# RetNet attention and a gated FFN on one core: the first batch's state is moved between partitions by two matrix products instead of two DMA copies

## The chip, the cores and the metric

The kernel runs on one core of a Trainium2 chip. A core has five instruction streams that run side by side and wait for each other through semaphores: TensorE (PE in the profile), VectorE (DVE), ScalarE (ACT), GpSimd (POOL) and SyncE (SP, which here only issues DMAs). Sixteen DMA engines move data between the chip's memory (HBM) and SBUF, the on-chip memory of 128 partitions. Matrix products are written to PSUM, which has eight banks.

The metric is device time in microseconds (us), as the median of several executions. Less is better.

## The reference

The reference computes a parallel RetNet attention for 8 batches of 8 heads (576 positions, 64 values per head), lays the result out as 4608 tokens of 512 values, and sends these through a gated feed-forward layer:

```python
def _attn_ref(q, k, v) -> np.ndarray:
    B, H, S, D_ = q.shape
    scale = 1.0 / np.sqrt(D_)
    scores = scale * np.matmul(q, k.transpose(0, 1, 3, 2))
    gamma = 1.0 - 2.0 ** (-5.0 - np.arange(H, dtype=np.float32))
    ...
    Dmat = np.where(rel >= 0, gamma[:, None, None] ** rel[None, :, :], 0.0)
    ret = scores * Dmat[None, :, :, :]
    return np.matmul(ret, v).astype(np.float32)
    ...
def _moe_ref(x, w_gate, w_val, w_out) -> np.ndarray:
    gate = 1.0 / (1.0 + np.exp(-(x @ w_gate)))
    val = x @ w_val
    return (gate * val @ w_out).astype(np.float32)
```

The feed-forward layer is 512 to 1536 to 512. The decay `gamma ** (i - j)` splits into a factor of the query's position and one of the key's, so attention can be done in chunks: inside a chunk by masked scores, and across chunks by a running state per head, the sum of k times v so far (64 x 64 values).

## The kernel before

**Attention.** The first chunks of batches 0 and 1 are done as "pairs" of 256 positions (`PAIRS`); everything after that as "steps" of 128 positions (`STEPS`), each of which loads `k`, `q` and `v` (256 KB each, lines 170 and 173), scales and casts them to bf16 (`cast_qk`, `cast_v`), turns q and k with a transposing DMA (`cross`, line 420), and makes scores (`scores`, L640), new shares of the state (`products`, L648), and values (`intra`, L666, and `inter`, L681, which multiplies by the state). A batch's last 64 positions are joined with those of the next batch in one step, in which `inter` reads the state of both batches after four chunks.

Batch 0's state is kept differently from the others'. The pairs keep it as a block matrix `sbd`: head 2m stands in partitions 0 to 63 and columns 0 to 63 of block m, head 2m+1 in partitions 64 to 127 and columns 64 to 127, with zeros elsewhere. The steps want head y*4+m in partitions half(y) and block m. `first_batch_state` makes the second form from the first, in a tile named `sf` in the profile: two quarters stay in their partitions and are copied by ACT, and two quarters change partitions and are copied by a DMA each, one issued on SP and one on ACT. It is called in `next_slot` for step 1. The step that reads the result is the last of batches 0 and 1, several steps later.

**Feed-forward.** The first 512 tokens are done while the weights still land (`h_both`, L1315, then `op_first`, L1465), the next 512 in two blocks of 256 (`h_units`, L884, `op_units`, L1225), and the other 3584 in blocks of 512 with a seven-product scheme (L1008 and L1123). The work of attention is put between the feed-forward products in an order that the kernel writes out by hand; each engine runs its list in order.

**Loads.** All loads go through a ring of landing tiles of 2 KB per partition (`landing`), and nearly all are issued on SP. The loads of pairs are in pieces of 512 bytes in SBUF, those of steps in pieces of 256 bytes (one head of one position), those of weights in pieces of 512 bytes for the first four, 1024 for the next four, and 2048 for the other sixteen and for `wo`. The order of issue in the first stage is: pairs 0 and 1, the gate and value weights, two loads of `wo`, `k` and `q` of pair 2, six of `wo`, `v` of pair 2 (`v32p`), four of `wo`. POOL casts that `v` into `vp` (L395), and TensorE's `pair_st` (L478) reads it.

**Places in SBUF.** Pools are laid out in the order in which they are opened. `lead` is the first and holds `blank`, `sbd[0]`, `trip` and `tri`, 1920 bytes per partition, from byte 16512 on; the landing tiles follow from byte 18432, and then all other pools; `consts` is the last.

Of the kernel before, what the change touches and what calls it, by code (L numbers as in the profile page):

```python
# [9 lines left out]
FP32 = mybir.dt.float32  # L10
BF16 = mybir.dt.bfloat16
# [5 lines left out]
def kernel(  # L17
# [19 lines left out]
    nc = tc.nc  # L37

    B, H, S, D = q.shape
    NT, DM = out.shape  # L40
    DFF = moe_w_gate.shape[1]
    P = 128
    M = H // 2
# [4 lines left out]
    lead = ctx.enter_context(tc.tile_pool(name="lead", bufs=1))  # L48
# [13 lines left out]
    st_psum = ctx.enter_context(tc.tile_pool(name="st_psum", bufs=1, space=PS))  # L62
# [44 lines left out]
    LAST = NC - 1  # L107
# [8 lines left out]
    NJ = P // 64  # L116
# [29 lines left out]
    def half(x):  # L146
        return slice(x * 64, x * 64 + 64)
# [16 lines left out]
    def load_part(s, i):  # L164

        b, c = STEPS[s]
        nm, src = (("k", k), ("q", q), ("v", v))[i]
        t = landing([P, H, D], f"{nm}32_{s}", s >= 8)
        if c < LAST:
            nc.sync.dma_start(out=t, in_=src[b, :, c * P:(c + 1) * P, :].rearrange("h p d -> p h d"))  # L170
        else:
            for j, (bj, tj) in enumerate(pieces_of(s)):
                nc.sync.dma_start(out=t[half(j)], in_=src[bj, :, tj:tj + 64, :].rearrange("h p d -> p h d"))
        loaded.setdefault(s, []).append(t)
# [93 lines left out]
    ident = consts.tile([P, P], BF16)  # L268
# [13 lines left out]
    sbd = [lead.tile([P, M, P], BF16, name="sbd0")]  # L282
# [6 lines left out]
    for p0 in (0, 64):  # L289
        nc.gpsimd.affine_select(out=trip[p0:p0 + 64], in_=trip[p0:p0 + 64], compare_op=ALU.is_ge, fill=0.0,  # L290
                                base=0, pattern=[[-1, 2], [1, P]], channel_multiplier=-2)
    tri = lead.tile([P, 64], BF16)

    def later_constants():

        nc.gpsimd.memset(tri, 1.0)
        for p0 in (0, 64):
            nc.gpsimd.affine_select(out=tri[p0:p0 + 64], in_=tri[p0:p0 + 64], compare_op=ALU.is_ge, fill=0.0,
                                    base=0, pattern=[[1, 64]], channel_multiplier=-1)
# [11 lines left out]
    on_pool, on_act, on_dve = nc.gpsimd.tensor_copy, nc.scalar.copy, nc.vector.tensor_copy  # L311
# [18 lines left out]
    def value_sums_begin():  # L330

        wt3_sb["w"] = []
        last = [sum_tile([P, 2, 2, 2 * P], BF16, f"wvt_{3 + i}", SUMS - 1 - i) for i in range(2)]
        for i in range(3):
            two = osb.tile([P, 2, 2, 2 * P], BF16, tag="osb", name=f"wvt_{i}")
            osb.held.append(osb.last)
            wt3_sb["w"].append([two[:, 0], two[:, 1], last[i // 2][:, i % 2]])
# [47 lines left out]
    def cast_pair(nm, A, g, eng):  # L385

        if (nm, A) not in natural:
            natural[nm, A] = osb.tile([P, 2, H, D], BF16, tag="osb", name=f"{nm}p_{A}")
        if nm != "v" and A == 2:
            o = natural[nm, A].rearrange("p r (m y) d -> p y m r d", y=2)[:, g]  # L390
        else:
            o = natural[nm, A][:, :, g * M:(g + 1) * M, :].rearrange("p r h d -> p h r d")
        i = parts.pop((nm, "pair", A, g))
        if nm == "v":
            eng(out=o, in_=i)  # L395
        else:
            tab = (ktab2 if nm == "k" else qtab2)[:, PAIRS[A][1], g * M:(g + 1) * M, :].unsqueeze(3).to_broadcast([P, M, 2, D])
            eng.tensor_tensor(out=o, in0=i, in1=tab, op=ALU.mult)
# [29 lines left out]
    state = {}  # L428
# [167 lines left out]
    def turn_step(s):  # L596

        t = att_pool.tile([P, 2, M, P], BF16, tag="T", name=f"T_{s}", bufs=6)
        for i, ((pool, tag), eng) in enumerate(zip(VALS, (on_act, on_dve))):
            ps = pool.tile([P, M, P], BF16, tag=tag, name=f"turn_{s}_{i}")  # L600
            for m in range(M):
                nc.tensor.matmul(ps[:, m, :], lhsT=natural_qk[s][:, i, m, :], rhs=ident, is_transpose=True,
                                 start=(m == 0), stop=(m == M - 1))
            eng(out=t[:, i], in_=ps)
        turned[s] = t
# [4 lines left out]
    def new_state(key, dt=BF16):  # L610
        final = dt == BF16 and key[1] == LAST - 1 and key[2] == NJ - 1
        tag = "s32" if dt == FP32 else "sf" if final else "sb"
        return nat_pool.tile([P, M, D], dt, tag=tag, name=f"{tag}_{key[0]}_{key[1]}_{key[2]}", bufs=8 if tag == "sb" else 5)

    def keep_state(key, src, eng):
        state[key] = new_state(key)
        eng(out=state[key], in_=src)  # L617
# [73 lines left out]
    def slot(s):  # L691

        if s > 0:
            val_ps[s - 1] = values(M, s - 1)
            intra(s - 1)
            inter(s - 1, [(0,), (1,)])
            mark(st_psum, "st")
        scores(s)
        if STEPS[s][1] < LAST:
            products(s)  # L700
        if s > 0:
            mark(st_psum, "st")
            inter(s - 1, [(1,), (0,)])
        mask(s)
# [74 lines left out]
    def after(s, i):  # L779

        makes = STEPS[s][1] < LAST
        to_bf16 = on_act if s < 6 else on_pool
        if i == 0:
            if makes:
                add_state(s, 0)
        else:
            if s > 0:
                leave_x(s - 1, i - 1)
                if i == 2 and dealt(cols_of(s - 1, 0)):
                    x_sums(at_col[s - 1], False)  # L790
            if i == 1 and makes:
                add_state(s, 1)
            if makes and (s, i - 1) in totals:
                b, c = STEPS[s]
                keep_state((b, c, i - 1), totals.pop((s, i - 1)), to_bf16)


    def first_batch_state():

        whole = new_state((0, LAST - 1, NJ - 1))  # L800
        for hh in range(2):
            for y in range(2):
                ((nc.sync, nc.scalar)[y].dma_start if hh != y else nc.scalar.copy)(
                    out=whole[half(y), hh::2, :], in_=sbd[3][half(hh), 2 * y:2 * y + 2, half(hh)])
        state[0, LAST - 1, NJ - 1] = whole

    pending = []

# [3 lines left out]
    def loads_to(n):  # L812
        while done["ld"] < min(3 * NS, n):
            load_part(*divmod(done["ld"], 3))
            done["ld"] += 1

    def casts_to(s):
        while done["cast"] <= min(NS - 1, s):
            x = done["cast"]
            loads_to(3 * (x + 1 + (AHEAD[x] if x < len(AHEAD) else 2)))  # L820
            cast_qk(x, 1, nc.gpsimd)
            cast_qk(x, 0, nc.vector if x < 2 else nc.gpsimd)
            if x not in TURNED:
                cross(x)
            cast_v(x, on_dve if x == 0 else on_pool)
            done["cast"] += 1
# [23 lines left out]

    def next_slot(s):
        slot(s)
        if s == 1:
            first_batch_state()
        casts_to(s + LEAD_CAST)
        for i in range(3):
            pending.append(lambda i=i: after(s, i))
        if s + 1 == 1:
            pending.insert(2, lambda: turn_step(s + 1))
# [463 lines left out]
    def step(units, n):  # L1323
        for _ in range(n):
            next(units)
# [88 lines left out]
    for i in range(2):  # L1414
        cast_w("g", 2, 2, i, on_pool)
    later_constants()
    cast_w("v", 2, 2, 0, on_pool)
    for i in range(4):
# [34 lines left out]
    step(units, 2)  # L1453
    cast_pair("q", 2, 1, nc.vector)
    step(units, 2)
    loads_to(6)
    value_sums_begin()
    for u in range(2):
# [65 lines left out]
    for w, (t0, n) in enumerate(BLOCKS):  # L1524
# [18 lines left out]
        for i, cols in enumerate(ffn_units(t0, n, nxt)):  # L1543
            if i in SUMS_AT.get(w, ()) and weight_sums:
                weight_sums.pop(0)()
            if w == 1 and i == n_h + TURN_AT:
                turn_step(7)
            for x in SPARE.get((w, i - n_h if w == 1 else i), ()):
                x()
            gone += cols  # L1550
            pieces += 1
            if stores and (nxt is None or w + 2 == len(BLOCKS) and pieces % 4 == 0):
                leave()
            if n > 256 and i % 2 and i < n_h:
                continue
            if pending:
                pending.pop(0)()
            elif slots < end and gone * (end - begin) >= (slots - begin) * (total - 5 * 2048):
                next_slot(slots)
                valued = slots - 1  # L1560
                slots += 1
            elif twos and (cue if n == 512 else i - n_h >= 1):
                cue.clear()
                next_two(*twos[0], n == 512)
                valued = twos[0][0][-1]
                slots = max([slots] + [s + 1 for s in twos.pop(0)[1]])
# [34 lines left out]
```

## Time and profile before

| | |
|---|---|
| median of 3 runs | 307.34 us (306.61 to 311.28) |
| the profiled execution | 309.1 us, of which the span of the instructions is 307.4 us |
| busy: PE, DVE, ACT, POOL | 298.5, 245.7, 196.9, 207.7 us |
| bytes moved by DMA | 55.01 MB, 179 GB/s over the span |
| granted clock of TensorE | 1.0 |

A row of a timeline gives the start and the duration in us, the engine, the line, the operation, the tiles written and read, and in square brackets the idle time of the engine before it and what ended it. "SPq" and "ACTq" are the engines' DMA issues. A row of the windows gives the stretch, its length, the busy time of PE, PEld, DVE, ACT and POOL with the number of instructions, the granted clock, the DMA share, and GB/s.

### The profile page before, as it was taken

The numbers are of one execution on the slowest core, as the hardware profiler recorded it, in microseconds if no ns is written. First come the engines' busy times: TensorE is split into PE (matmuls) and PEld (weight loads), VectorE is DVE, ScalarE is ACT, GpSimd is POOL, SyncE is SP. The second block draws the span as 40 slices with busy tenths as digits, with TensorE's granted clock in tenths as the row PEclk, the third lists the DMA queues.
The fourth block names the chain that finished last, engine by engine and source line by source line (L and its number), as shares of the span: only waits on it lengthen the run. The fifth ranks groups of instructions, "written<-read, shape, count | busy, mean of one in ns | idle before, by whom it ended". The sixth has DMA issues, their size and how long they took to land.

```text
span 307.4 us, 10860 instructions
## 1 busy us (share of the span) xinstructions
PE 298.5 (97%) x4442; PEld 244.2 (79%) x4442; DVE 245.7 (80%) x476; ACT 196.9 (64%) x422; POOL 207.7 (68%) x255
## 2 busy tenths in 40 slices
PE   8899999999999999999999999999999999999994
PEld 7774455876858788888888888888888888888883
DVE  5857695766889899789978997898789968945893
ACT  6765354454547746974797479757965796658640
POOL 5676463745476699769976997699669916751490
PEclk9999999999999999999999999999999999999999
DMA  7999999999999971999599919992880282013004
GB/s 211 315 295 393 341 322 229 216 200 180 228 202 263 227 167 38 233 231 231 133 226 254 177 38 214 228 211 41 211 200 2 61 282 75 2 52 90 0 3 137
DMA packets 144994, 55.01 MB, mean 179 GB/s; under 512 B 124336, under 2 KB 136880, under 8 KB 144944
## 3 DMA queue, kind: packets, MB, share of 16 engines
q1 hardware_dynamic: 144000, 53.64, 73.1%
q8 instruction: 35, 0.57, 0.8%
q10 hardware_dynamic: 944, 0.67, 0.8%
q14 instruction: 15, 0.12, 0.1%
HBM read 37.75 MB, written 9.44 MB: 154 GB/s over the span
## 4 chain that ended last, share of the span: by engine, by line
PE 68%; DMA 14%; DVE 8%; SPq 5%; issue 2%; POOL 1%; ACT 1%; ACTq 0%; DVEq 0%; POOLq 0%
PE gatea L1008 11%; PE wa L1008 10%; PE qa L1123 10%; PE qe L1123 7%; PE we L1008 5%; PE gatee L1008 5%; PE op L1225 3%; DMA wg<-in_moe_w_gate_dram 3%; SPq L184 3%; PE gateg L1008 3%; DMA q<-in_q_dram 3%; PE wg L1008 3%; DMA q32p<-in_q_dram 2%; PE h_v L884 2%; PE h_g L884 2%; DMA v32p<-in_v_dram 2%
## 5 line engine op out<-in xcount | busy, mean ns | idle before, releaser
L411 POOL TENSOR_TENSOR qk<-k,ktab 128x512 bf16<-128x512 f32 x30 | 32.2, 1073 | 16.0 <-DMA k<-in_k_dram 13.1
L1008 PEld LDWEIGHTS <-wg_sb 128*128 128x128 bf16 x336 | 32.8, 98 | 4.3
L1008 PEld LDWEIGHTS <-wv_sb 128*128 128x128 bf16 x336 | 32.9, 98 | 4.1 <-issue 0.3
L1123 PEld LDWEIGHTS <-gsum 128*128 128x128 bf16 x336 | 32.0, 98 | 4.9 <-DVE gsum L945 0.6
L945 POOL TENSOR_TENSOR gsum<-gv 128x256 bf16<-128x256 bf16 (+1 forms) x34 | 25.9, 769 | 12.4 <-DVE gv L1033 11.3
L411 POOL TENSOR_TENSOR qk<-q,qtab 128x512 bf16<-128x512 f32 x28 | 31.4, 1121 | 1.3 <-DMA q<-in_q_dram 1.3
L1008 PEld LDWEIGHTS <-wvt 128*128 128x128 bf16 x252 | 24.6, 98 | 3.9 <-issue 0.9
L1008 PEld LDWEIGHTS <-wgt_sb 128*128 128x128 bf16 x252 | 24.6, 98 | 3.7 <-issue 0.8
L1033 POOL TENSOR_TENSOR gv<-gv,wu 128x512 bf16<-128x512 bf16 x7 | 8.1, 1164 | 27.9 <-DVE wu L1059 27.9
L945 POOL TENSOR_TENSOR gsum<-gv,gsum 128x256 bf16<-128x256 bf16 x39 | 26.9, 720 | 0.0
L655 DVE TENSOR_TENSOR pt<-row,tri 128x256 bf16<-128x256 f32 x60 | 21.4, 412 | 6.6 <-PE val L681 3.1
L1123 PEld LDWEIGHTS <-gv 128*128 128x128 bf16 x240 | 23.0, 98 | 3.4 <-issue 0.4
L1008 PE MATMUL wa<-xsum,wv_sb 128*128 128x256 bf16 x168 | 25.2, 273 | 0.1
L1008 PE MATMUL gatea<-xsum,wg_sb 128*128 128x256 bf16 x168 | 24.1, 273 | 0.0
L617 ACT CAST sb<-s 128x256 bf16<-128x256 f32 x46 | 18.3, 413 | 6.3 <-DVE s L774 4.8
L742 ACT CAST xT<-val 128x256 bf16<-128x256 f32 x50 | 15.8, 388 | 6.6 <-PE val L681 6.6
L939 POOL TENSOR_TENSOR gsum<-gv 128x256 bf16<-128x256 bf16 (+1 forms) x16 | 14.5, 909 | 7.8 <-DVE gv L1033 7.8
L1054 DVE TENSOR_TENSOR gatee<-gatea,gs 128x512 f32<-128x512 f32 x14 | 9.8, 698 | 10.7 <-PE gatea L1008 7.4
L1033 POOL TENSOR_TENSOR gv<-gv,ws 128x512 bf16<-128x512 bf16 x14 | 16.3, 1164 | 2.6 <-DVE ws L1062 2.6
L1031 ACT ACTIVATE gv<-gs 128x512 bf16<-128x512 f32 x21 | 13.0, 630 | 7.8 <-DVE gs L1062 7.8
L1062 DVE TENSOR_TENSOR gs<-gatea,gs 128x512 f32<-128x512 f32 x21 | 13.8, 686 | 4.4 <-PE gatea L1008 3.6
L1062 DVE TENSOR_TENSOR ws<-wa,ws 128x512 f32<-128x512 f32 x21 | 14.4, 684 | 3.7 <-PE wa L1008 3.7
(181 smaller groups left out, 853.5 us busy)
## 6 DMA issues: line engine op xcount, KB each, us to landing
k<-in_k_dram SPq DMA_DIRECT2D x26, 256.0 KB, 4.2
q<-in_q_dram SPq DMA_DIRECT2D x26, 256.0 KB, 4.1
v<-in_v_dram SPq DMA_DIRECT2D x26, 256.0 KB, 4.3
out_dram<-ob SPq DMA_DIRECT2D x25, 256.0 KB, 3.1
wg<-in_moe_w_gate_dram SPq DMA_DIRECT2D x12, 256.0 KB, 5.1
wv<-in_moe_w_val_dram SPq DMA_DIRECT2D x12, 256.0 KB, 5.2
wo<-in_moe_w_out_dram SPq DMA_DIRECT2D x12, 256.0 KB, 5.1
v32p<-in_v_dram SPq DMA_DIRECT2D x6, 256.0 KB, 5.4
```

Of the source, the lines that this page charges most:

```text
L411: eng.tensor_tensor(out=natural_qk[s][:, i].rearrange("p m (y d) -> p y m d", y=2), in0=by_halves(loaded[s][1 - i]), in1=tab, op=ALU.mult)
L617: eng(out=state[key], in_=src)
L655: nc.vector.tensor_tensor(out=probs[s][:, y], in0=row_ps[s][y][:, 0], in1=tri.unsqueeze(1).to_broadcast([P, M, 64]), op=ALU.mult)
L742: nc.scalar.copy(out=x_out(ALL, cols_of(s, i)), in_=x_in(val_ps[s][i], cols_of(s, i)))
L884: nc.tensor.matmul(ps[:, i], lhsT=w_sb[:, kc, (fc + i) * P:(fc + i + 1) * P], rhs=xT(kc, slice(t0, t0 + n)), start=(kc == 0), stop=(kc == ...
L939: eng.tensor_tensor(out=s3, in0=a11, in1=a21, op=ALU.subtract)
L945: eng.tensor_tensor(out=to, in0=a, in1=b, op=op)
L1008: nc.tensor.matmul(ps[:, f], lhsT=w[:, kc, f * P:(f + 1) * P], rhs=x[:, kc], start=(first and f == 0 and kc == 0), stop=(f == 1 and kc == ...
L1031: nc.scalar.activation(out=to, in_=src, func=AF.Sigmoid)
L1033: eng.tensor_tensor(out=to, in0=to, in1=src, op=ALU.mult)
L1062: nc.vector.tensor_tensor(out=me["s5"], in0=a, in1=me["s5"], op=ALU.add)
L1123: nc.tensor.matmul(ps[:, b], lhsT=left(fp)[:, b * P:(b + 1) * P], rhs=right(fp), start=(first and fp == 0 and b == 0), stop=(fp == NFC // ...
```

## The change

A constant `stacked` of 128 x 192 is made on POOL in `later_constants`: zeros, with a 64 x 64 unit matrix in columns 64 to 127 of both halves of the partitions. Its columns 64 to 191 hold the unit matrices on the left (they add both halves of the input's partitions into the upper half of the output's), its columns 0 to 127 on the right (into the lower half). Two products with these, which add up in one PSUM tile `whole`, move the four quarters of `sbd[3]` to their places; the zeros of the block matrix add nothing. One ACT cast makes the bf16 tile `sf` of it. The function is called earlier: in the first 512 tokens, behind the last `h_both`, instead of in step 1.

```diff
     tri = lead.tile([P, 64], BF16)
+    stacked = lead.tile([P, 192], BF16)
 
     def later_constants():
 
+        nc.gpsimd.memset(stacked, 0.0)
+        for hh in range(2):
+            nc.gpsimd.tensor_copy(out=stacked[half(hh), 64:128], in_=ident[half(hh), half(hh)])
         nc.gpsimd.memset(tri, 1.0)
...
     def first_batch_state():
 
-        whole = new_state((0, LAST - 1, NJ - 1))
-        for hh in range(2):
-            for y in range(2):
-                ((nc.sync, nc.scalar)[y].dma_start if hh != y else nc.scalar.copy)(
-                    out=whole[half(y), hh::2, :], in_=sbd[3][half(hh), 2 * y:2 * y + 2, half(hh)])
-        state[0, LAST - 1, NJ - 1] = whole
+        ps = st_psum.tile([P, M, D], FP32, tag="st", name="whole")
+        for y in range(2):
+            nc.tensor.matmul(ps, lhsT=stacked[:, P - 64 * (y + 1):2 * P - 64 * (y + 1)], rhs=sbd[3][:, 2 * y:2 * y + 2, :],
+                             start=(y == 0), stop=(y == 1))
+        keep_state((0, LAST - 1, NJ - 1), ps, on_act)
...
         slot(s)
-        if s == 1:
-            first_batch_state()
         casts_to(s + LEAD_CAST)
...
     cast_pair("q", 2, 1, nc.vector)
     step(units, 2)
+    first_batch_state()
     loads_to(6)
     value_sums_begin()
```

With `stacked`, `lead` holds 2304 bytes, and the landing tiles begin at byte 18816 of each partition; all other tiles of the later pools move up by the same 384 bytes.

On ACT in step 1 before the change: the two copies of quarters, with the DMA issue between them, stand between the casts of the states `sb` and the sigmoid `gv`.

```order
L617 COPY sb_2_1_1263<-s_1_2_1_1224 128x256
L803 COPY sf_3_1_1353<-sbd_293 64x2x64
L803 DMA sf_3_1_1353<-sbd_293 64x2x64
L803 COPY sf_3_1_1353<-sbd_293 64x2x64
L887 ACTIVATE gv_1_1252<-h_g_6_1371 128x2x256
L762 COPY xT_1393<-val_0_1276 128x4x64
```

After the change the three are gone from there, and one cast stands much earlier on ACT, in the first 512 tokens, between the cast of a `wo` weight and the copies of pair 2's turned `k` and `q`:

```order
L318 COPY wo_sb<-wo_3_187 128x512
L621 COPY sf_3_1_856<-whole 128x256
L452 COPY kT_890<-kTp_0_885 128x512
L452 COPY qT_898<-qTp_0_893 128x2x2x128
L452 COPY kT_890<-kTp_1_902 128x512
L452 COPY qT_898<-qTp_1_910 128x2x2x128
```

So ACT loses two copies and a DMA issue in step 1 and has one cast more ahead of the four `kT` and `qT` copies. On SP in step 1 before the change, the other DMA copy stands between the transpose and the loads of step 5:

```order
L420 DMA_TRANSPOSE T_1197<-qk_1194 128x8x128
L803 DMA sf_3_1_1353<-sbd_293 64x2x64
L170 DMA k_5_1358<-in_k_dram 128x8x64
L170 DMA q_5_1360<-in_q_dram 128x8x64
L170 DMA v_5_1362<-in_v_dram 128x8x64
```

After the change the loads follow the transpose at once; nothing is put in the place of the DMA. On TensorE after the change, the two products stand behind the last product of `h_both` (`hv_11`) and ahead of the first of `op_first`:

```order
L1316 MATMUL hv_11_847<-xT_536,wv_sb 128x512
L806 LDWEIGHTS stacked
L806 MATMUL whole<-sbd_293,stacked 128x256
L806 LDWEIGHTS stacked
L806 MATMUL whole<-sbd_293,stacked 128x256
L1467 LDWEIGHTS gv_0_623
L1467 MATMUL op_0_881<-wo_sb,gv_0_623 128x512
```

Nothing else moves on TensorE. The line numbers after the change are up to 4 higher than before.

## The prediction

> **What bounds the kernel now.** I read the page's first two parts, then the windows by stage, the chain of waits, and the timelines around the two places that the change touches.
>
> ```profile
> PE 298.5 (97%) x4442; PEld 244.2 (79%) x4442; DVE 245.7 (80%) x476; ACT 196.9 (64%) x422; POOL 207.7 (68%) x255
> DMA  7999999999999971999599919992880282013004
> ```
>
> TensorE is busy for 97% of the span, so removing waits can win little. In the left third of the DMA row, up to about slice 14 of 40 (110 us), the DMA engines are as full as TensorE. The windows say this with numbers; the last two columns are the DMA share (mean busy share of 16 engines; overlapping packets can push it above 1) and GB/s.
>
> ```profile
> 1.00:19.00 18.00, 16.63 (x298) 14.04 (x299) 13.96 (x39) 12.36 (x24) 10.96 (x20) 1.00 0.96 282
> 19.00:45.00 26.00, 25.14 (x180) 12.84 (x179) 19.02 (x36) 13.66 (x26) 15.83 (x26) 1.00 1.02 347
> 60.00:88.00 28.00, 27.73 (x547) 20.92 (x537) 21.10 (x47) 12.74 (x31) 15.17 (x18) 1.00 1.10 205
> 5.00:10.00 5.00, 4.37 (x86) 3.66 (x86) 3.10 (x6) 3.05 (x6) 2.35 (x3) 1.00 1.10 321
> 25.00:30.00 5.00, 5.00 (x25) 2.25 (x23) 3.40 (x8) 3.51 (x6) 2.30 (x4) 1.00 1.06 404
> 80.00:85.00 5.00, 5.00 (x93) 4.51 (x79) 3.88 (x9) 2.47 (x6) 2.79 (x4) 1.00 1.09 246
> ```
>
> From 1 to 45 us the share is 0.96 and 1.02: no free DMA time. Where TensorE needs something that lands last in this stage, it waits, and the row shows it:
>
> ```profile
> 42.73 1.37 POOL L395 CAST vp<-v32p 128x512 bf16<-128x512 f32 x2 [0.58 <-DMA v32p<-in_v_dram]
> 43.40 0.19 PE L478 MATMUL st<-vp,kp 64*64 64x64 bf16 x1
> 44.15 0.31 PE L478 MATMUL st<-vp,kp 64*64 64x64 bf16 x9 [0.56 <-POOL vp L395]
> ```
>
> So until 44 us the end is set by how fast bytes land, after that by TensorE with the DMA close behind. The granted clock is 1.00 in every window.
>
> **The change, the small terms.** *TensorE.* Two products of 256 columns are added behind the last `hv`. From the chain of waits, and the timelines of TensorE and ACT:
>
> ```profile
> 81.41 0.87 PE h_g L884 x8
> 42.69 0.64 PE L457 MATMUL qkp<-qT,kT 64*64 64x128 bf16 x32
> 38.80 0.62 ACT L314 CAST wo_sb<-wo 128x512 bf16<-128x512 f32 x1 [3.42 <-DMA wo<-in_moe_w_out_dram]
> 40.86 0.76 ACT L448 COPY qT<-qTp 128x512 bf16<-128x512 bf16 x1
> ```
>
> Eight such products take 0.87 us, so two take 0.22. They stand ahead of the wait of 0.56 us for `vp` at 43.40, which covers them: 0. Without that cover they cost 0.22. *ACT there.* The new cast of `whole` is queued behind the `wo` cast that ends at 39.42 and ahead of four copies of `kT` and `qT`. From the page's groups, POOL's groups and POOL's timeline:
>
> ```profile
> L617 ACT CAST sb<-s 128x256 bf16<-128x256 f32 x46 | 18.3, 413 | 6.3 <-DVE s L774 4.8
> 20.30 0.52 POOL L298 TENSOR_SCALAR_AFFINE_SELECT tri<-tri 64x64 bf16<-64x64 bf16 x2
> L288 POOL MEMSET trip<- 128x256 bf16 x1 | 0.3, 337 | 0.0
> 22.89 1.23 POOL L309 CAST wg_sb<-wg 128x512 bf16<-128x512 f32 x2 [0.76 <-DMA wg<-in_moe_w_gate_dram]
> ```
>
> A cast of this shape takes 0.41, so the last copy ends at 42.03 instead of 41.62, still before the products at 42.69 that read it: 0. *POOL.* A memset of 192 columns (the 256-column one took 0.34) and two copies of 64x64 (the row of two 64x64 selects took 0.52): at most 0.9 us at 20.07. POOL then waits 0.76 us for a weight at 22.13, so at most 0.14 us is handed on, and the casts behind it wait for DMA again; should the cover fail, 0.9 us less the 0.56 at `vp` is 0.3. *The old place.* Here the change takes something away; timelines of ACT, TensorE and SP:
>
> ```profile
> 59.40 0.30 ACT L803 COPY sf<-sbd 64x128 bf16<-64x128 bf16 x1
> 61.04 0.71 ACTq L803 DMA_DIRECT2D sf<-sbd  x1
> 61.79 0.29 ACT L803 COPY sf<-sbd 64x128 bf16<-64x128 bf16 x1 [2.10 <-DMA T<-qk]
> 63.31 0.59 ACT L887 ACTIVATE gv<-h_g 128x512 bf16<-128x512 f32 x1
> 63.80 0.36 ACT L762 CAST xT<-val 128x256 bf16<-128x256 f32 x1
> 61.84 1.04 PE L884 MATMUL h_g<-xT,wg_sb 128*128 128x256 bf16 x8
> 63.72 0.22 PE L666 MATMUL val<-pt,v 64*64 64x64 bf16 x2
> 64.21 0.31 PE L666 MATMUL val<-pt,v 64*64 64x64 bf16 x14 [0.27 <-ACT xT L762]
> 64.59 0.73 SPq L803 DMA_DIRECT2D sf<-sbd  x1
> 65.42 0.53 SPq L170 DMA_DIRECT2D k<-in_k_dram  x1
> ```
>
> ACT's DMA issue could not go out until an earlier transposing DMA had landed (the 2.10 us at 61.79), and everything on ACT stood behind it. TensorE felt 0.49 us of that (63.72 to 64.21, where its neighbours start 0.02 apart). Without it the `gv` of 63.31 waits only for its `h_g`, which ends at 62.88, and starts at about 62.95; `xT` behind it is then 0.36 us earlier: -0.36 us. SP is freed of 0.83 us (64.59 to 65.42), and all later loads and transposes go out that much earlier.
>
> So the edits as written give 307.34 - 0.36 = **307.0 us**. That would be the forecast but for one thing that the diff moves without naming it.
>
> **The term that decides: where every tile lies.** `stacked` (192 columns of 2 bytes, 384 bytes per partition) is allocated in `lead`, the first pool. All tiles of the later pools move up by 384 bytes. Before, the landing tiles begin at byte 18432, a multiple of 256; after, at 18816, which is 128 more than a multiple of 256. The same holds for `qk`, `T`, `ob` and every other tile that a DMA reads or writes. The pieces that DMAs move are 256 bytes (`k`, `q`, `v` by head, the transposes), 512, 1024 or 2048 bytes, and each of them now lies across one 256-byte border more than before.
>
> What does a border cost? No DMA of this trace with pieces of 256 bytes or more starts off such a border, so it is bounded. The windows above give the price of a piece: 16 engines x share x size / rate. 2048 bytes (25 to 30 us, weights): 16 x 1.06 x 2048 / 404 = 86 ns. 512 bytes (5 to 10 us): 28 ns. 256 bytes (80 to 85 us): 18.1 ns. That is a straight line, 8.4 ns for a piece and 9.7 ns for each 256-byte block. If the 9.7 ns is paid for bytes moved, a border costs nothing. If it is paid for each block touched, a piece that straddles pays one block more: 256 bytes then cost 27.8 ns, what the 512-byte row costs for the same two blocks. Below nothing I exclude: no piece touches fewer blocks than before. I take the middle, half a block, 4.85 ns, because a straddling piece resembles the 512-byte row in the blocks touched and the 256-byte row in the bytes moved; both ends stay in the range.
>
> [...]
>
> *First stage.* These loads of 256 KB are ahead of the `vp` that TensorE waits for: 22 in pieces of 512 bytes (11264), 4 of 1024 (1024), 24 of 2048 (3072), together 15360 pieces. 15360 x 4.85 / 16 engines = **4.7 us** later, on a share of 1.0, with nothing free to hide it; that much later TensorE goes on from 44.15. With a whole block it is 9.3.
>
> *Steps.* Each step loads `k`, `q`, `v` and transposes: 4 x 1024 pieces of 256 bytes. From the instructions of L640 between 50 and 82 us, those on `T` between 66 and 75, and the timelines:
>
> ```profile
> L640 PE MATMUL row<-T x96: 192/193/213, 54.1 to 80.0; 64*64 64x64 bf16 x96
> 67.67 1.69 SPq L420 DMA_TRANSPOSE T<-qk  x1
> DMA to landing us min/median/max: 4.5/5.1/5.7
> 73.80 0.20 PE L640 MATMUL row<-T 64*64 64x64 bf16 x2
> 79.85 0.20 PE L640 MATMUL row<-T 64*64 64x64 bf16 x2
> ```
>
> TensorE takes six steps in that row, five intervals from 54.1 to 79.85: 5.15 us a step. The DMA needs 4096 x 18.1 / 16 = 4.63 us a step now, 5.88 at half a block, 7.1 at a whole one. So at half a block the DMA sets the pace, 0.73 us a step. The cover is thin: the transpose issued at 67.67 lands 5.7 us later, at 73.37, and is read at 73.80, 0.43 us of slack; SP's 0.83 us add to that. Five steps: 5 x 0.73 - 1.26 = **2.4 us**. From about 88 us on, steps are made in pairs, and the loads run far ahead (the DMA share falls to 0.01 at 115 us); I count nothing there. The 0.36 us at 64 us are not won in this case, because ACT's wait is replaced by later transposes.
>
> Sum: 4.7 + 2.4 = 7.1 us. The profiled execution took 309.1 us (span 307.4 and 1.7 around it), so it would take 316.2; the median of the runs shown, 307.34, lies 1.8 lower: **314.4 us, 2.3% slower**. About 2% (6.1 us, so 313.5 us) is what a measurement of this kernel can tell from no change.
>
> **Rivals.**
> - *Borders cost nothing, or only where SBUF is read.* Then the edits as written count: 307.0 us, not slower. If transposes alone pay, 1024 x 4.85 / 16 = 0.3 us a step makes 4.94, still under 5.15, and the time is 307.1. It decides in favour of this from the price at which a step fits: (5.15 x 16 / 4096 - 0.0181) us = 2.0 ns a border, with the first stage then at +1.9 us at most. For it: the straight line of the prices passes through pieces of one to eight blocks, so a further block in a row has no start-up price of its own beside its bytes. Against: the share is 1.0 throughout the first stage, so any price at all shows. 0.37.
> - *A border costs a whole block.* 9.3 us in the first stage, and 5 x (7.1 - 5.15) - 1.26 = 8.5 in the steps: 309.1 + 17.8 = 326.9 in the profile, 325 us as a median. For it: the 512-byte row. Against: half the bytes. 0.13.
> - *POOL or ACT late in the weight stage.* The 0.9 us of POOL reach TensorE, or the cast on ACT delays the products at 42.69: up to +0.3 us and the 0.36 not won, 307.3 to 308. 0.05.
> - *Faster by over 2%.* TensorE would have to lose 6 us of waits, where its idle time over the whole span is 307.4 - 298.5 = 8.9 us, and the waits touched here come to 0.5. 0.02.
>
> **How the numbers follow.** The forecast, a border at a price between 3 and 7 ns, has 0.43, its own range 311 to 319 us; a fifth of that (0.08) lies under 313.5. Slower by over 2%: 0.35 + 0.13 and 0.02 for what I overlook = 0.50. Within 2%: 0.08 + 0.37 + 0.05, less the 0.02 = 0.48. Faster: 0.02. The range 306.5 to 323 takes in the rival at 307 and leaves out the upper part of the whole-block case and the lowest runs of the first rival, about 0.15 together.
>
> **What would show it.** In the windows 5 to 10, 25 to 30 and 80 to 85 us: the same share at less GB/s (270, 380 and 195 for the half block) if borders cost; the old prices of 28, 86 and 18 ns if not. The `vp` row at 42.73 at 47.4 or at 42.7. A wait for a transposing DMA ahead of L640 (L644 after) in the steps. If the first rival holds: the idle 0.27 at 64.21 gone, TensorE's other rows 0.3 us earlier and the rest alike. I am wrong in kind if the DMA prices are unchanged and the time still moves by more than 1 us, or if `whole` on TensorE or ACT turns up in the chain of waits.

## The result, and the profile after

| | before | after |
|---|---|---|
| median of 6 runs each | 308.29 us (306.61 to 311.28) | 311.25 us (310.5 to 312.72) |
| ratio | | 1.011, 95% interval 1.0075 to 1.0144 |
| the profiled execution | 309.1 us, span 307.4 | 310.5 us, span 308.7 |

The changed kernel is slower, by 1.1%: a loss that is clear of zero, and half of the 2.3% that was forecast. This ratio and all later ones leave out runs over 1.5% above the fastest of the same kernel, here the 311.28 us of before. The profiled executions are only 1.4 us apart, because the one of before lies 0.8 us above its median and the one of after 0.75 below. The traces therefore show about half of the 3.0 us between the medians.

The page of after: the engine totals, and the queue that carries loads, stores and transposes (packets, MB, share of 16 engines' time).

```profile
PE 298.6 (97%) x4444; PEld 243.9 (79%) x4444; DVE 246.3 (80%) x476; ACT 196.7 (64%) x421; POOL 208.7 (68%) x258
...
q1 hardware_dynamic: 143856, 53.63, 79.4%
```

The same queue before:

```profile
q1 hardware_dynamic: 144000, 53.64, 73.1%
```

TensorE does the same work. The queue moves the same bytes in the same pieces (144 fewer, those of the DMA copy that was issued on SP), yet its packets take 79.4% instead of 73.1% of the engines' time. So a piece seems to cost more, as the deciding term said. The windows of after that answer to those of before:

```profile
19.00:45.00 26.00, 25.44 (x184) 13.09 (x183) 18.63 (x36) 14.31 (x28) 16.65 (x29) 1.00 1.04 348
5.00:10.00 5.00, 4.06 (x83) 3.49 (x84) 3.01 (x6) 2.98 (x6) 2.09 (x2) 1.00 1.15 303
25.00:30.00 5.00, 5.00 (x25) 2.25 (x23) 3.19 (x7) 2.89 (x5) 2.94 (x5) 1.00 1.05 387
80.00:85.00 5.00, 4.78 (x105) 4.23 (x106) 4.17 (x9) 2.30 (x6) 2.43 (x3) 1.00 1.25 184
```

Where 270, 380 and 195 GB/s were expected at an unchanged share, there are 303, 387 and 184 at shares of 1.15, 1.05 and 1.25. By the same formula a piece of 512 bytes now costs 16 x 1.15 x 512 / 303 = 31.1 ns (28 before) and one of 2048 bytes 88.9 (86). One of 256 bytes comes to 16 x 1.25 x 256 / 184 = 27.8 ns (18.1), which is what the prediction's whole block would cost; a kernel that only moves bytes, below, shows less, so this formula is no price at full speed. But from 19 to 45 us the rate is 348 GB/s against 347: **dearer pieces, and nearly the same bytes at the same time**. How late TensorE gets its data is the next thing to read. Windows of the first 130 us, before and then after:

```profile
0.00:45.00 45.00, 41.77 (x476) 26.88 (x477) 33.10 (x77) 26.02 (x49) 27.10 (x49) 1.00 0.97 313
45.00:100.00 55.00, 54.60 (x874) 39.99 (x873) 42.29 (x86) 28.58 (x65) 30.68 (x33) 1.00 1.10 219
100.00:130.00 30.00, 29.12 (x475) 25.43 (x475) 26.66 (x49) 21.31 (x49) 25.48 (x29) 1.00 0.73 166
```

```profile
0.00:45.00 45.00, 40.96 (x476) 26.18 (x477) 32.55 (x76) 26.10 (x50) 27.63 (x51) 1.00 1.02 312
45.00:100.00 55.00, 54.78 (x872) 40.09 (x871) 41.69 (x88) 28.68 (x65) 28.15 (x30) 1.00 1.12 197
100.00:130.00 30.00, 28.54 (x470) 24.56 (x468) 26.63 (x47) 19.78 (x45) 28.27 (x32) 1.00 1.01 184
```

Length less PE busy is TensorE's idle time. It was 3.23, 0.40 and 0.88 us, and is 4.04, 0.22 and 1.46: 1.21 us more in all, which is nearly the whole difference of the spans (1.3). Nothing more is lost later: from 130 to 290 us TensorE is busy for all of the 160 us in both. TensorE's timeline of after names the waits:

```profile
44.51 0.41 PE L482 MATMUL st<-vp,kp 64*64 64x64 bf16 x15 [0.51 <-POOL vp L399]
...
80.56 0.32 PE L644 MATMUL row<-T 64*64 64x64 bf16 x16 [0.22 <-DMA T<-qk]
...
116.22 1.05 PE L1124 MATMUL qa<-wt_sb,gsum 128*128 128x256 bf16 x8 [0.70 <-POOL gsum L946]
```

The products on `vp` go on at 44.51 instead of 44.15: 0.36 us late, not 4.7. One step waits for its transposing DMA, by 0.22 us. The largest new wait, 0.70 us for POOL's sums `gsum`, stands where the prediction counted nothing. POOL's timeline ahead of it, from 100 us on, before and then after:

```profile
100.62 1.16 POOL L1033 TENSOR_TENSOR gv<-gv,wu 128x512 bf16<-128x512 bf16 x1 [2.15 <-DVE wu L1059]
```

```profile
100.72 0.61 POOL L420 CAST v<-v 128x512 bf16<-128x512 f32 x1 [1.06 <-DMA v<-in_v_dram]
101.97 1.04 POOL L415 TENSOR_TENSOR qk<-k,ktab 128x512 bf16<-128x512 f32 x1 [0.63 <-PE gatea L1009]
...
104.24 1.16 POOL L1034 TENSOR_TENSOR gv<-gv,wu 128x512 bf16<-128x512 bf16 x1
```

Before, POOL had its casts behind it at 100 us and waited 2.15 us for VectorE. After, it still has casts of steps ahead of it, waits 1.06 us for a load of `v`, and comes to the same `gv` product 3.6 us later, without a wait of its own. So in this execution the late loads seem to reach TensorE through POOL's queue, at a place where the prediction looked for nothing.

### The profile page after: what moved, and what is told of

Read it like the earlier page. It is cut to its first block, busy times and chain, and to the rows that moved or that the text cites. A ratio compares the mean times of both kernels' runs of the same rounds, so it can differ in the third digit from the quotient of the medians.

```text
span 308.7 us, 10863 instructions
## 1 busy us (share of the span) xinstructions
PE 298.6 (97%) x4444; PEld 243.9 (79%) x4444; DVE 246.3 (80%) x476; ACT 196.7 (64%) x421; POOL 208.7 (68%) x258
## 3 DMA queue, kind: packets, MB, share of 16 engines
q1 hardware_dynamic: 143856, 53.63, 79.4%
## 4 chain that ended last, share of the span: by engine, by line
PE 67%; DMA 14%; SPq 8%; POOL 5%; DVE 3%; issue 2%; ACT 0%; POOLq 0%; DVEq 0%
PE gatea L1009 10%; PE qa L1124 10%; PE wa L1009 10%; PE qe L1124 8%; PE we L1009 5%; PE gatee L1009 5%; DMA wg<-in_moe_w_gate_dram 3%; SPq L184 3%; DMA k<-in_k_dram 3%; POOL gsum L946 3%; PE gateg L1009 2%; PE wg L1009 2%; PE op L1467 2%; PE h_v L885 2%; PE h_g L885 2%; DMA q32p<-in_q_dram 2%
```

## The experiments

**Is it the place of the tiles, or the edit?** First the change with `stacked` in the last pool, so that no DMA tile moves:

```diff
-    stacked = lead.tile([P, 192], BF16)
+    stacked = consts.tile([P, 192], BF16)
```

> The changed kernel with `stacked` taken from the last pool instead of the first, so that every tile that a DMA reads or writes begins on a 256-byte border again, as before. Theory of the borders: the whole loss goes, and only the edits as written are left, a ratio to the kernel before of 0.999 (-0.36 us of 308.3); DMA prices as before the change (80 to 85 us near 18 ns a piece of 256 bytes). Rival, the edits themselves (products on TensorE, constants on POOL, the earlier cast): the ratio stays at 1.01, as after the change.

Measured: 308.19 against 308.0 us, ratio 1.0009 (0.9977 to 1.0041). Then the place alone, with the kernel before and an unused tile in `lead`, of 384, 128, 256 and (in a later series) 64 bytes:

```diff
     tri = lead.tile([P, 64], BF16)
+    gap = lead.tile([P, 192], BF16, name="gap")
```

> The kernel before with an unused tile of 384 bytes per partition in `lead`: no instruction changes, all later tiles move up as in the change. Theory of the borders: slower by as much as the change plus the 0.36 us that the edits win, a ratio of 1.011 to 1.013, with the DMA prices of the changed kernel. Rival, the edits: 1.000.

> The kernel before with an unused tile of 128 bytes in `lead`: tiles begin 128 bytes past a 256-byte border, as with 384. Theory of the borders at 256 bytes: the same ratio as with 384 bytes, 1.01. Rival, that something else of the 384 counts (the offset within 512 or 2048 bytes): another ratio than with 384.

> The kernel before with an unused tile of 256 bytes in `lead`: tiles move off the 512-byte and 2048-byte borders but still begin on a 256-byte border. Theory of borders at 256 bytes: 1.000 and the old DMA prices. Rival, borders at 512 or 2048 bytes: 1.01, as with 384 bytes.

> The kernel before with 64 unused bytes in `lead`: pieces of 256 bytes straddle a border as with 128, but in parts of 192 and 64 bytes. If each border has a price of its own, the same ratio as with 128 bytes, 1.012 to 1.018; if the price goes with the smaller or the larger part, clearly less or more than with 128.

| unused bytes | past a 256-byte border | ratio to before | 95% interval |
|---|---|---|---|
| 384 | 128 | 1.0135 | 1.0083 to 1.0186 |
| 128 | 128 | 1.0179 | 1.0125 to 1.0232 |
| 256 | 0 | 1.0026 | 0.9994 to 1.0057 |
| 64 | 64 | 1.0162 | 1.0111 to 1.0212 |

An unused tile makes the whole loss. The 256 bytes cost nothing measurable, though tiles then lie off borders of 512 bytes: of the offsets tried, only those that leave the borders of 256 bytes cost time. 64 bytes past it cost what 128 cost. And the edits as written, with the tiles where they were, make no measurable difference.

**Who pays, the writer or the reader of SBUF?** A second gap of 128 bytes behind the landing tiles brings the rest (`qk`, `T`, `ob`) back to its borders, or, alone, moves only the rest:

```diff
     ld_pool = ctx.enter_context(tc.tile_pool(name="ld", bufs=12))
+    behind = ctx.enter_context(tc.tile_pool(name="behind", bufs=1))
...
     tri = lead.tile([P, 64], BF16)
+    gap = lead.tile([P, 64], BF16, name="gap")
+    gap_behind = behind.tile([P, 64], BF16, name="gap_behind")
```

> The kernel before with 128 unused bytes ahead of the landing tiles and 128 behind them: only the landing tiles begin off a 256-byte border, so only the loads, which write into SBUF, straddle; `qk`, `T` and `ob` lie as before. If the writing side pays: the ratio of the kernel with 128 bytes ahead of everything, 1.01 to 1.018, and the load queue's share of the DMA engines near 79% instead of 73%. [...]

> The kernel before with 128 unused bytes behind the landing tiles only: the loads lie as before, and the transposes (which read `qk` and write `T`) and the stores (which read `ob`) straddle. If the writing side of the loads pays: at most 1.003 and a share of 73 to 75%. If the reading side pays: 4.85 ns on each of 1024 pieces of a transpose, a share near 75 to 76%, and a ratio up to 1.01 where a step waits for its transpose.

With only the landing tiles off their borders the ratio is 1.0146 (1.0094 to 1.0198). With only the rest off (the same, without `gap`) it is 0.9981 (0.9948 to 1.0013). The loads make the whole loss; what transposes and stores lose in this kernel can't be measured. It is not the engines that read the landing tiles: POOL's products of `k` take 1073 ns before and 1090 with gap_landing, those of `q` 1121 and 1108 ns. One expectation failed: the load queue's share came to 74.4% with gap_landing, where 79% was expected (73.3% with gap_rest). It is 76.0, 79.7 and 83.0% with gaps of 384, 128 and 64 bytes, so the share does not follow the loss.

**What does a border cost?** A kernel that only moves bytes, eight DMAs of 256 KB a stage, into tiles on a border and 128 bytes past one:

> The disputed cost by itself. This kernel leaves out the whole computation: it only moves bytes, in stages that wait for each other, eight DMAs of 256 KB a stage. Loads with pieces of 256, 512, 1024 and 2048 bytes go into tiles that begin on a 256-byte border (on) and 128 bytes past one (off), each size on, off, on, off; then stores of 2048-byte and of 256-byte pieces out of the on tiles and out of the off tiles, and transposes. Theory: the price is a fixed 2 to 4 ns for a piece that is written across one border more, so off costs 20 to 22 instead of about 18 ns a piece of 256 bytes, 30 to 31 instead of 28 ns of 512, and at most 3% more for 1024 and 2048 bytes; stores cost the same on and off. First rival (the prediction's): 4.85 ns for every piece that straddles, so 23 and 33 ns, and 91 instead of 86 at 2048. [...]

After each DMA, VectorE clears a column of its tile, so its rows tell when DMAs have landed. Rows of three pairs of stages (on, off), the first and the last that count for the price: 512 bytes loaded, 2048 loaded, 2048 stored:

```profile
53.33 0.18 DVE L65 MEMSET on<- 128x1 f32 x2 [0.48 <-DMA on<-in_q_dram]
...
58.58 0.18 DVE L65 MEMSET on<- 128x1 f32 x2 [0.61 <-DMA on<-in_q_dram]
59.51 0.18 DVE L65 MEMSET off<- 128x1 f32 x2 [0.75 <-DMA off<-in_q_dram]
...
64.86 0.18 DVE L65 MEMSET off<- 128x1 f32 x2 [0.70 <-DMA off<-in_q_dram]
...
99.89 0.18 DVE L65 MEMSET on<- 128x1 f32 x2 [0.45 <-DMA on<-in_moe_w_out_dram]
...
104.29 0.18 DVE L65 MEMSET on<- 128x1 f32 x2 [0.45 <-DMA on<-in_moe_w_out_dram]
104.97 0.18 DVE L65 MEMSET off<- 128x1 f32 x2 [0.49 <-DMA off<-in_moe_w_out_dram]
...
109.59 0.18 DVE L65 MEMSET off<- 128x1 f32 x2 [0.46 <-DMA off<-in_moe_w_out_dram]
110.25 0.18 DVE L65 MEMSET on<- 128x1 f32 x2 [0.48 <-DMA out_dram<-on]
...
114.84 0.18 DVE L65 MEMSET on<- 128x1 f32 x2 [0.47 <-DMA out_dram<-on]
115.49 0.18 DVE L65 MEMSET off<- 128x1 f32 x2 [0.47 <-DMA out_dram<-off]
...
120.07 0.18 DVE L65 MEMSET off<- 128x1 f32 x2 [0.49 <-DMA out_dram<-off]
```

In these stages, whose DMAs overlap with those of the stage ahead, the 256-byte rows were uneven (0.77 to 2.05 us between the landings of the first off stage), and the last five of eight 256-byte stores out of the off tiles ran slower than the first three (1.19 to 1.26 us apart, after 0.91 and 0.93). So the 256-byte pieces, an offset of 64 bytes, and the transposes were measured again, a stage starting when the one ahead has landed:

> Again only DMAs, with the whole computation left out, and now with stages that do not overlap: a stage of eight DMAs starts when the last DMA of the stage before has landed. Loads of 256-byte and of 512-byte pieces into tiles on a border, 128 bytes past one and 64 bytes past one; then stores of 256-byte pieces out of tiles on a border and 128 bytes past one; then six transposes a stage, on and 128 bytes past. Theory: loads pay for a straddle and 64 bytes past costs what 128 bytes past costs, 1.5 to 2.5 ns a piece of 256 bytes and 3.5 to 4.5 of 512; stores and transposes read SBUF at the same speed on and off. Rival: reading pays too, and the 256-byte stores take 2 to 4 ns more a piece out of the off tiles in both of their stages, as the last five of eight did in the first kernel of this kind; transposes are then longer by at least 5%.

256-byte loads off by 128, on, and off by 64 (on: the undisturbed landings of the stage, since transposes ran in between), then 256-byte stores on and off:

```profile
42.06 0.06 DVE L59 MEMSET off<- 128x1 f32 x1 [1.16 <-DMA off<-in_k_dram]
...
46.88 0.06 DVE L59 MEMSET off<- 128x1 f32 x1 [1.15 <-DMA off<-in_k_dram]
...
70.04 0.06 DVE L59 MEMSET on<- 128x1 f32 x1 [1.72 <-DMA on<-in_k_dram]
70.91 0.06 DVE L59 MEMSET on<- 128x1 f32 x1 [0.81 <-DMA on<-in_k_dram]
71.80 0.06 DVE L59 MEMSET on<- 128x1 f32 x1 [0.84 <-DMA on<-in_k_dram]
...
95.61 0.06 DVE L59 MEMSET off<- 128x1 f32 x1 [1.15 <-DMA off<-in_k_dram]
...
100.43 0.06 DVE L59 MEMSET off<- 128x1 f32 x1 [1.15 <-DMA off<-in_k_dram]
...
193.23 0.06 DVE L59 MEMSET on<- 128x1 f32 x1 [0.83 <-DMA out_dram<-on]
...
198.66 0.06 DVE L59 MEMSET on<- 128x1 f32 x1 [0.84 <-DMA out_dram<-on]
...
202.91 0.06 DVE L59 MEMSET off<- 128x1 f32 x1 [1.11 <-DMA out_dram<-off]
...
208.99 0.06 DVE L59 MEMSET off<- 128x1 f32 x1 [1.16 <-DMA out_dram<-off]
```

A price is 16 engines x time / pieces. In the second kernel a DMA has 1024 pieces: two DMAs land between 70.04 and 71.80, four between 42.06 and 46.88 and between 95.61 and 100.43, six from 193.23 to 198.66, five from 202.91 to 208.99. In the first kernel the stretches shown are seven DMAs each (six for 512 bytes off; with the last landing, which came sooner, it would be 27.3 ns), of 512 pieces of 512 bytes or 128 of 2048. So 512 bytes on a border cost 16 x 5.25 us / (7 x 512) = 23.4 ns.

| ns a piece | on a border | past one | difference |
|---|---|---|---|
| load, 256 bytes | 13.8 | 18.8 (128 and 64 past) | 5.0 |
| load, 512 bytes | 23.4 | 27.9 | 4.5 |
| load, 2048 bytes | 78.6 | 82.5 | 3.9 |
| store, 256 bytes | 14.1 | 19.0 | 4.9 |
| store, 2048 bytes | 82.0 | 81.8 | none |

The 13.8 ns of the 256-byte loads is the least sure of these: it rests on two landings. All eight of that stage, with transposes between them, land 1.13 us apart on average, and the eight of the second stage on borders of the first kernel, without transposes, 1.12 us: 17.6 ns a piece. What held up the others is not known. So 5.0 ns is the difference between even landings, and over whole stages it is smaller.

My theory for the first kernel, a fixed 2 to 4 ns and at most 3% for long pieces, fell (5.0 and 4.5 ns, and 5% at 2048 bytes), and so did that for the second, 1.5 to 2.5 ns at 256 bytes and nothing for stores. The prediction's own price, 4.85 ns for every straddling piece, holds on the loads within 1 ns at all three sizes. Reading pays too, where pieces are of 256 bytes: 19.0 instead of 14.1 ns, a third more. Loads into SBUF pay as much (18.8 instead of 13.8 ns); for stores of 2048 bytes the runs show no such loss (81.8 and 82.0 ns). This kernel's stores are of long pieces. For the transposes the medians from issue to landing were 3.0 on and 3.2 us off in the first kernel, 3.2 and 3.8 in the second, there beside unequal loads: they seem to pay, by how much stays open, and the ratio of 0.9981 above says that this kernel doesn't feel it.

**Does ACT's wait for a transpose cost more when loads are late?** The gap of 384 bytes showed something that the changed kernel does not have. Its timelines of ACT and of TensorE, and its window of 60 to 88 us:

```profile
65.79 0.71 ACTq L804 DMA_DIRECT2D sf<-sbd  x1
66.54 0.29 ACT L804 COPY sf<-sbd 64x128 bf16<-64x128 bf16 x1 [6.08 <-DMA T<-qk]
```

```profile
67.51 1.14 PE L885 MATMUL h_v<-xT,wv_sb 128*128 128x256 bf16 x8 [3.87 <-ACT gv L888]
```

```profile
60.00:88.00 28.00, 24.00 (x478) 17.92 (x477) 16.18 (x36) 10.49 (x27) 13.71 (x15) 0.94 1.02 183
```

Around its DMA issue, which the change removes, ACT is idle for 6.08 us instead of 2.10: 0.71 us of each is the issue itself, the rest (5.3 and 1.3 us) the wait for the transpose. TensorE stands for 3.87 us behind it, the granted clock of the stretch is 0.94, and eight products of `h_g` take 1.84 us at 70.06 where they took 1.04 at 62.60. It is not always so. With loads on their borders this idle time of ACT is 2.7 us (gap256) and 2.8 (gap_rest), and TensorE's longest wait behind it 0.64; past borders it is 2.6 us with 128 bytes, 3.3 with 64 and 5.1 with gap_landing, and TensorE waits 0.35, 1.1 and 2.8. So late loads can make this wait long, as in two traces of four. Then both DMA copies were issued on SP, with the tiles on and off their borders:

```diff
-                ((nc.sync, nc.scalar)[y].dma_start if hh != y else nc.scalar.copy)(
+                (nc.sync.dma_start if hh != y else nc.scalar.copy)(
```

> Before, with both DMA copies of the state issued on SP, so that ACT waits for no earlier transpose. Theory: without the wait of 2.1 us on ACT, TensorE wins about 0.3 us there, which can't be told from nothing in the time: ratio 0.998 to 1.002. Rival: the wait on ACT is worth more than it shows, ratio under 0.995.

> The same with 384 unused bytes in the first pool, so that all later tiles lie where they lie after the change. Theory: what gap384 and gap128 lost beyond the changed kernel is ACT's wait for a late transposing DMA at its own DMA issue (6.1 us, with 4 us of TensorE idle and a stretch at half clock). With the issue on SP that is gone: no idle of 4 us on TensorE between 58 and 70 us, no half clock in the window 60 to 88, and a ratio of 1.008 to 1.012, as the changed kernel has. Rival: the extra loss is the loads' alone, the ratio is 1.013 to 1.018 as with the gaps.

On their borders: 308.26 against 308.49 us, ratio 0.9968 (0.9926 to 1.001), which can't be told from no change. With the gap: 1.0115 (1.0076 to 1.0154), and in the trace the clock of the window is 1.00 again. The window, and TensorE's two longest waits between 45 and 130 us:

```profile
60.00:88.00 28.00, 26.40 (x502) 20.31 (x488) 20.29 (x43) 12.73 (x32) 13.81 (x15) 1.00 1.05 172
```

```profile
75.52 0.32 PE L641 MATMUL row<-T 64*64 64x64 bf16 x16 [0.98 <-DMA T<-qk]
...
118.23 1.05 PE L1124 MATMUL qa<-wt_sb,gsum 128*128 128x256 bf16 x8 [1.16 <-POOL gsum L946]
```

The long stall is gone, as expected, but three steps wait for their own transposing DMA (0.25, 0.98 and 0.38 us). In the time the ratio of 1.0115 is the changed kernel's 1.011, but its interval overlaps that of gap384, so the gain is shown in the trace and not in the time. That the four kernels with the issue on ACT and loads past borders lie higher, at 1.0135 to 1.0179, points the same way. The wait on `gsum` near 116 to 118 us is there in the changed kernel, with the gaps of 128 and 64 bytes (0.58 and 0.57 us) and here (1.16), all with loads off their borders. It is absent in all five traces with loads on their borders, and in the two (384 bytes, landing tiles alone) in which TensorE had already lost 2.8 us or more to ACT's wait.

No version beat the kernel before: the edits are worth nothing that can be measured, and the tiles lay on their borders to begin with.

## Why the prediction was right or wrong

**The mechanism was right.** The loss is made by where the tiles lie, not by the edits: 1.0009 without the shift, 1.0135 with the shift alone. The first rival, that only the reading side pays, fell with gap_landing and gap_rest. The price of a border was right too: 4.85 ns taken, 3.9 to 5.0 measured on loads. It was taken as the middle between two bounds, so the close fit is in part luck.

**What was mis-sized is what the price does to the time.** Two terms, one error: a time per piece, or a share, read off a window and taken for full speed.

*First stage, +4.7 us.* The failed step is "on a share of 1.0, with nothing free to hide it". Measured are 0.36 us at `vp`, and 0.81 us more idle time of TensorE up to 45 us. The other traces agree: this idle time is 2.8 to 3.5 us in the five with loads on their borders and 3.8 to 4.1 in the six past them, 0.7 us more on average. The engines were not full. At the full-speed prices of the table the 15360 pieces need (11264 x 23.4 + 1024 x 41.8 + 3072 x 78.6) / 16 = 34.2 us on their borders and 38.4 past them (41.8, and 46.1 past, for 1024 bytes, from the straight line between 512 and 2048). The last of these loads lands at 42.6 us (issued at 37.24, 5.34 us to landing, by the chain of before). So there was room for both. A share of 1.0 looked full, but packets overlap, and the share goes above it (1.13 and 1.06 here). Windows of the first byte-moving kernel at full speed on its borders, loads of 512 and of 2048 bytes (busy time of VectorE and POOL, clock, share, GB/s):

```profile
40.00:44.00 4.00, 0.60 (x11) 0.00 (x0) 1.00 1.13 339
...
90.00:94.00 4.00, 0.77 (x13) 0.00 (x0) 1.00 1.06 407
```

Full is 339 to 407 GB/s at shares of 1.06 to 1.13, where the kernel before has 282 at 0.96 and 347 at 1.02. What filled the rest is in the waits of SP's queue up to 45 us, before and then after (its longest on an engine: us in total, times, longest us):

```profile
SPq L197 <- POOL wg_sb L309: 2.1, 2, 1.8
SPq L203 <- POOL wo_sb L314: 1.5, 1, 1.5
```

```profile
SPq L184 <- POOL wv_sb L313: 1.3, 1, 1.3
```

These are loads that wait for casts to free landing tiles: 3.6 us in the two longest of before, 1.3 in the longest of after, and 6.3 and 4.2 us in all such waits on engines. So a slower DMA could use up part of such waits here: they are 2.1 us shorter after, and the rate from 19 to 45 us is the same (348 and 347 GB/s). The windows show the catching up: from 19 to 25 us the changed kernel moves 383 GB/s where before had 319. That these waits cover all of the missing 4 us was not shown by a run of its own; they vary between kernels.

```profile
19.00:25.00 6.00, 6.00 (x38) 3.47 (x37) 3.21 (x7) 3.23 (x8) 4.89 (x11) 1.00 1.02 319
```

```profile
19.00:25.00 6.00, 5.95 (x38) 3.46 (x37) 2.62 (x7) 3.69 (x9) 5.05 (x14) 1.00 1.06 383
```

*Steps, +2.4 us.* The failed step is the 18.1 ns that was taken as the full-speed price of a 256-byte piece, with 4.85 on top of it: 22.95 ns, where a piece past a border is measured at 18.8 (and one on a border at 13.8 to 17.6). If the transposes' pieces cost what those of loads cost, 4096 pieces take 4.8 us a step past borders, under the 5.15 us of TensorE, so the DMA does not set the pace. "2.0 ns a border" as the point from which a step fits fell with the same 18.1. The changed kernel's trace has one wait for a transpose, the 0.22 us at 80.56, and gap256, on its borders, has much the same:

```profile
80.63 0.32 PE L641 MATMUL row<-T 64*64 64x64 bf16 x16 [0.23 <-DMA T<-qk]
```

But a transpose can land late at this price: with the issues on SP and the tiles past borders, such waits come to 1.6 us, and without the shift to none. TensorE's idle time from 45 to 100 us is 0 to 0.9 us in the five traces on borders and 0.2 to 4.0 in the six past them, so the term is not nothing; it varies from kernel to kernel.

*What came later.* "I count nothing there" was wrong in the other direction: 0.58 us more idle time from 100 to 130 us, mostly behind POOL, which gets its loads late.

**The small terms.** Two products, one cast and POOL's preparations are covered as argued: `whole` and `stacked` are in no wait, and the copies of `kT` and `qT` still end ahead of the wait for `vp`. The idle 0.27 at 64.21, less than the 0.36 that was counted for it, is gone in the changed kernel. It is gone with stacked_last as well, but there TensorE waits 0.63 us at 59.70 for VectorE, and is idle from 45 to 100 us for 0.76 us, where it was 0.40 before. So the -0.36 us is not shown, neither in the traces nor in the time (1.0009 and 0.9968).

**The range and the chances.** 311.25 us lies in the range and in the forecast's own range, at its lower end, between the two cases that held most of the chance: a border costs what the forecast took, but most of it is hidden, and the time moves toward that of the first rival, in which a border costs nothing. The range, 306.5 to 323 us, holds both, so that the time lies in it says little; the cause and the price of a border were foreseen, and where the loss would arise was not.

## What to carry to other kernels

A diff that adds a tile to an early pool moves every later tile: look at what the new size does to the borders of tiles that DMAs write, and put odd sizes last (here a ratio of 1.0009) or pad them to 256 bytes (1.0026, where 64, 128 and 384 bytes cost 1.0135 to 1.0179). Don't take a DMA share near 1 as full, nor a window's time per piece as the full-speed price, before a kernel that only moves bytes has shown what full is: here 282 GB/s at a share of 0.96 and 347 at 1.02 were not full, 339 at 1.13 and 407 at 1.06 were. When transfers get slower, follow the slack engine by engine: here part of the loss turned up on TensorE behind POOL, 0.70 us at 116.22, some 70 us after the first stage.

## What the runs showed that I had not expected

A piece pays the same for lying 64 as for lying 128 bytes past a border (18.8 ns each, ratios 1.0162 and 1.0179 to 1.0135): so, of the two offsets tried, the border that is crossed counts and not the bytes beyond it. Between even landings it is much the same for pieces of 256 and of 2048 bytes written into SBUF (5.0 and 3.9 ns), while stores that read 2048-byte pieces out of SBUF pay nothing (82.0 ns on a border, 81.8 past one).

The edit may have a value that depends on the layout. ACT stood idle around its DMA issue for 2.1 to 2.8 us with loads on their borders and for 2.6 to 6.1 past them, and at 6.08 TensorE waited 3.87 us and the granted clock of the window was 0.94. By removing that issue the change can save itself from part of the harm that it does by moving the tiles; the traces show this, the times don't yet.
